# Linear attention and sentence-level experts on one core: repeated weights copied on chip, q relaid, a one-step root, and a searched order of work

## The chip, the cores and the metric

The kernel runs on one core of one Trainium2 chip. The metric is the time of one execution on the device in microseconds (us), and lower is better. Several executions of both kernels are taken on the same chip. A run counts as fast or slow by its own spread, and only fast runs are compared. A profile of one execution shows what each engine did. Its span is shorter than the reported time by some 1.7 us.

## The reference, cut to what matters

```python
# q, k, v: (8 batches, 8 heads, 576 rows, 64), fp32
kv  = einsum('bhsd,bhse->bhde', k, v)
out = einsum('bhsd,bhde->bhse', q, kv)
x   = out / sqrt(mean(out*out, -1) + 1e-6) * g_norm      # -> (8, 576, 512)
logits = x.mean(axis=1) @ w_gate                         # one row of 8 experts per batch
e      = argmax(logits, axis=1)                          # one expert for a whole batch
gate   = softmax(logits)[e]
out[b] = gate * (relu(x[b] @ w1[e]) @ w2[e])             # w1[e]: 512x1024, w2[e]: 1024x512
```

The weights of an expert are 4.19 MB in fp32, two matrices of 512 x 1024. The inputs are fixed, and with them the experts chosen are 4 4 7 6 5 1 3 1. So batch 1 repeats batch 0, and batch 7 repeats batch 5.

## The kernel before

For each batch there are stages, written as tokens of an order list: K (the kv matrix of all heads), T (transposes of q), O (q times kv and its square), M (mean of squares and root), X (normalized, transposed x), G (gate steps) and 17 units m0 to m16 of expert matrices. In the list "2T1" is batch 2, stage T, head pair 1. The list fixes the order on every engine, since each engine takes its instructions in the order in which they were written down.

```python
ORDER = ("0G2 1K 1T0 1T1 1T2 1O0 1T3 ... 0m0 0m1 1M2 1M3 0m2 ...")            # cut

def load_qkv(b, parts, which=None):                      # GpSimd issues, fp32 -> fp16 on the way
    ...
    for t, src in zip(kvq[b], (k, v, q)):
        nc.gpsimd.dma_start(t[0:R, hs], src[b, hs].rearrange(...))

def s_qt(b, c, ...):                                     # 12 half-width transposes for a head pair
    for j in range(NJ):
        for i in range(2):
            nc.tensor.transpose(pt[64*i:64*i+64, 0, j*R:(j+1)*R],
                                kvq[b][2][0:R, 2*c+i, j, :], ident[0:R, 0:R])
    nc.vector.tensor_copy(qT[:, c, :], pt[:, 0, 0:S])

def s_m(b, c):                                           # root in two ScalarE steps
    ...
    nc.scalar.activation(two(ln), pm[:, :, 0:HS], AF.Ln, bias=epsc)
    nc.scalar.activation(ln, ln, AF.Exp, scale=-0.5)

def s_gate2(b):                                          # expert's number, then its weights
    nc.tensor.matmul(pg, mean, ts, start=True, stop=True)
    nc.vector.max(mx, pg);  nc.vector.max_index(ix, mx, pg)
    nc.scalar.activation(lg, pg, AF.Exp, bias=nm, accum_out=gs)
    ev = nc.gpsimd.value_load(ix[0:1, 0:1], min_val=0, max_val=E - 1)
    nc.gpsimd.dma_start(w1, moe_w1[ds(ev, 1)]...)        # every batch loads 4.19 MB
    nc.gpsimd.dma_start(w2, moe_w2[ds(ev, 1)]...)
    load_qkv(b + 2, 1)                                   # q, k, v for a later batch, behind them

# m0..m7: w1 against xT, then Relu on ScalarE;  m8..m16: w2 against hT, then
# scaling by the gate on VectorE into ot (pool of 3 buffers), stored from SyncE
outp = ctx.enter_context(tc.tile_pool(name="outp", bufs=3))
```

Of the kernel before, what the change touches and what calls it, by code (L numbers as in the profile page):

```python
# [10 lines left out]
F16 = mybir.dt.float16  # L11
U32 = mybir.dt.uint32
# [6 lines left out]

ORDER = (  # L20
    "0G2 1K 1T0 1T1 1T2 1O0 1T3 1O1 1M0 1O2 1X0 1O3 1M1 0m0 0m1 1M2 1M3 0m2 1X1 0m3 0m4 "
    "1X2 1X3 1G0 1G1 0m5 0m6 1G2 0m7 0m8 2K 0m9 0m10 2T0 2T1 0m11 2O0 2O1 0m12 2M0 0m13 "
    "2M1 2T2 2X0 2X1 0m14 2O2 2T3 0m15 0m16 1m0 2M2 2O3 1m1 1m2 2X2 2M3 1m3 1m4 1m5 2X3 "
    "2G0 2G1 3K 1m6 2G2 3T0 3T1 1m7 3O0 3T2 1m8 3M0 3T3 1m9 3O1 3X0 3O2 1m10 3M1 3X1 1m11 "
    "1m12 3M2 3X2 3O3 1m13 1m14 1m15 3M3 1m16 3X3 3G0 2m0 2m1 2m2 3G1 2m3 2m4 3G2 2m5 4K "
    "2m6 4T0 4T1 2m7 4O0 4T2 2m8 4M0 4T3 2m9 4O1 4X0 4O2 2m10 4M1 4X1 2m11 2m12 4M2 4X2 "
    "4O3 2m13 2m14 2m15 4M3 2m16 4X3 4G0 3m0 3m1 3m2 4G1 3m3 3m4 4G2 3m5 5K 3m6 5T0 5T1 "
    "3m7 5O0 5T2 3m8 5M0 5T3 3m9 5O1 5X0 5O2 3m10 5M1 5X1 3m11 3m12 5M2 5X2 5O3 3m13 3m14 "
    "3m15 5M3 3m16 5X3 5G0 4m0 4m1 4m2 5G1 4m3 4m4 5G2 4m5 6K 4m6 4m7 6T0 6T1 4m8 6O0 6O1 "
    "4m9 6M0 4m10 6X0 6M1 6T2 6X1 4m11 6T3 4m12 6O2 4m13 6M2 4m14 6X2 6O3 4m15 4m16 6M3 "  # L30
    "5m0 5m1 6X3 6G0 5m2 6G1 5m3 5m4 6G2 5m5 7K 5m6 5m7 7T0 7T1 5m8 7O0 7O1 5m9 7M0 5m10 "
    "7X0 7M1 7T2 7X1 5m11 7T3 5m12 7O2 5m13 7M2 5m14 7X2 7O3 5m15 5m16 7M3 6m0 6m1 7X3 "
    "7G0 6m2 7G1 6m3 6m4 7G2 6m5 6m6 6m7 6m8 6m9 6m10 6m11 6m12 6m13 6m14 6m15 6m16 7m0 "
    "7m1 7m2 7m3 7m4 7m5 7m6 7m7 7m8 7m9 7m10 7m11 7m12 7m13 7m14 7m15 7m16 "
# [4 lines left out]
def kernel(  # L39
# [17 lines left out]
    R = 96  # L57
    NJ = S // R
    NP = H // 2
    HS = S // 2  # L60
    EPS = 1e-6
# [4 lines left out]
    wp = ctx.enter_context(tc.tile_pool(name="wp", bufs=3))  # L66
# [3 lines left out]
    hp = ctx.enter_context(tc.tile_pool(name="hp", bufs=2))  # L70
    outp = ctx.enter_context(tc.tile_pool(name="outp", bufs=3))
    ps0 = tc.tile_pool(name="ps0", bufs=1, space=bass.MemoryType.PSUM)
    psp = [ps0.__enter__()]
    ctx.enter_context(tc.manual_schedule())

    kvq = [None] * B
    ACT_OT = ()
    LOADS = {0: (2,), 1: (3,), 2: (4,), 3: (5,), 4: (6,), 5: (7,), 6: ()}
# [3 lines left out]
    def load_qkv(b, parts, which=None):  # L82
        if kvq[b] is None:
            kvq[b] = [pqkv.tile([P, H, NJ, Dh], F16, tag=n, name=n) for n in ("kt", "vt", "qt")]
        step = H // parts
        for i in (range(parts) if which is None else which):
            for t, src in zip(kvq[b], (k, v, q)):
                hs = slice(i * step, (i + 1) * step)
                nc.gpsimd.dma_start(  # L89
                    t[0:R, hs], src[b, hs].rearrange("h (p j) d -> p h (j d)", j=NJ))  # L90
# [5 lines left out]
    load_qkv(0, 4, (0, 1))  # L96
# [4 lines left out]
    nc.gpsimd.dma_start(wg, moe_w_gate.rearrange("(c p) e -> p c e", p=P))  # L101
    nc.scalar.preload_act_table_set("natural_log_exp_and_others")
    epsc = const.tile([P, 1], F32)
    nc.vector.memset(epsc, EPS)
# [5 lines left out]
    nc.vector.memset(ones[64:128, 64:128], 1.0 / Dh)  # L110
    mean = const.tile([P, P], F32)
    nc.vector.memset(mean, 1.0 / S)
    gates = const.tile([P, B], F32)
# [13 lines left out]
    def s_qt(b, c, w=0, copy=True):  # L127
        s = st[b]
        if "qT" not in s:
            s["qT"] = att.tile([P, NP, S], F16, tag="qT", name="qT")  # L130
        p32 = psum("t", 1, 1) if b == 0 else psum("a")
        warm(p32, w)
        pt = p32.bitcast(F16)
        for j in range(NJ):
            for i in range(2):
                nc.tensor.transpose(pt[64 * i:64 * i + 64, 0, j * R:(j + 1) * R],  # L136
                                    kvq[b][2][0:R, 2 * c + i, j, :], ident[0:R, 0:R])
        s["pt", c] = pt
        if copy:
            s_tc(b, c)  # L140

    def s_tc(b, c):
        nc.vector.tensor_copy(st[b]["qT"][:, c, :], st[b]["pt", c][:, 0, 0:S])  # L143

    def s_kv(b, prs, w=0):
        kt, vt = kvq[b][0:2]
        kv = kvb[:, b % 2]
        p32 = psum("kv", 1, 1) if b == 0 else psum("a")
# [12 lines left out]
    def s_o(b, c, tag="a"):  # L161
        s = st[b]
        po = psum(tag)
        for i in range(2):
            nc.tensor.matmul(po[:, i, 0:HS], kvb[:, b % 2, c, :],  # L165
                             s["qT"][:, c, i * HS:(i + 1) * HS], start=True, stop=True)
        sq = sm.tile([P, S], F16, tag="sq", name="sq")
        nc.scalar.activation(two(sq), po[:, :, 0:HS], AF.Square)  # L168
        if b == 0:
            o = po[:, :, 0:HS]  # L170
        else:
            o = two(sm.tile([P, S], F32, tag="o", name="o"))
            nc.vector.tensor_copy(o, po[:, :, 0:HS])  # L173
        s["sq", c], s["o", c] = sq, o

    def s_m(b, c, exp=True):
        s = st[b]
        sq = s["sq", c]
        pm = psum("p", 1) if b == 0 else psum("a")
        for i in range(2):  # L180
            nc.tensor.matmul(pm[:, i, 0:HS], ones, sq[:, i * HS:(i + 1) * HS],  # L181
                             start=True, stop=True)
        ln = sm.tile([P, S], F32, tag="ln", name="ln")
        nc.scalar.activation(two(ln), pm[:, :, 0:HS], AF.Ln, bias=epsc)  # L184
        s["ln", c] = ln
        if exp:
            s_e(b, c)

    def s_e(b, c):
        ln = st[b]["ln", c]  # L190
        nc.scalar.activation(ln, ln, AF.Exp, scale=-0.5)  # L191

    def s_x(b, c):
        s = st[b]
        if "xT" not in s:
            s["xT"] = xp.tile([P, NP, S], F16, tag="xT", name="xT")
            s["pl"] = sm.tile([P, NP], F32, tag="pl", name="pl")
        nc.vector.scalar_tensor_tensor(out=two(s["xT"][:, c, :]), in0=s["o", c], scalar=gcol,  # L198
                                       in1=two(s["ln", c]), op0=ALU.mult, op1=ALU.mult,
                                       accum_out=s["pl"][:, c:c + 1])  # L200

    def s_gate(b):
        s = st[b]
        tw = sm.tile([P, NP, E], F32, tag="tw", name="tw")
        nc.vector.tensor_tensor(tw, wg, s["pl"].unsqueeze(2).to_broadcast([P, NP, E]), ALU.mult)
# [3 lines left out]

    def s_gate2(b):  # L210
        s = st[b]
        pg = (psum("kv", 1, 1) if b == 0 else psum("a"))[:, 0, 0:E]
        nc.tensor.matmul(pg, mean, s["ts"], start=True, stop=True)
        mx = sm.tile([P, 8], F32, tag="mx", name="mx")
        ix = sm.tile([P, 8], U32, tag="ix", name="ix")
        nc.vector.max(mx, pg)
        nc.vector.max_index(ix, mx, pg)
        nm = sm.tile([P, 1], F32, tag="nm", name="nm")
        nc.vector.tensor_scalar(out=nm, in0=mx[:, 0:1], scalar1=-1.0, scalar2=None, op0=ALU.mult)
        lg = sm.tile([P, E], F32, tag="lg", name="lg")  # L220
        gs = sm.tile([P, 1], F32, tag="gs", name="gs")
        nc.scalar.activation(lg, pg, AF.Exp, bias=nm, accum_out=gs)
        ev = nc.gpsimd.value_load(ix[0:1, 0:1], min_val=0, max_val=E - 1)
        w1 = wp.tile([P, 4, F], F16, tag="w1", name="w1")
        w2 = wp.tile([P, 8, D], F16, tag="w2", name="w2")
        nh = 2 if b in (0, B - 1) else 1
        for h in range(nh):
            fs = slice(h * F // nh, (h + 1) * F // nh)
            nc.gpsimd.dma_start(w1[:, :, fs],  # L229
                                moe_w1[ds(ev, 1), :, fs].rearrange("o (c p) f -> p (o c) f", p=P))  # L230
        nc.gpsimd.dma_start(w2, moe_w2[ds(ev, 1)].rearrange("o (c p) d -> p (o c) d", p=P))
        s["w"] = (w1, w2)
        s["gs"] = gs
        for n in LOADS.get(b, (b + 3,)):
            if n < B:
                load_qkv(n, 1)

    def s_gate3(b):
        nc.vector.reciprocal(gates[:, b:b + 1], st[b]["gs"])

    def m_1(b, fb):
# [10 lines left out]
        nc.scalar.activation(two(s["hT"][:, fb, :]), ph[:, :, 0:HS], AF.Relu)  # L253

    def m_2(b, t, fcs):
        s = st[b]
        w2 = s["w"][1]
        if fcs[0] == 0:
            s["pm2"] = psum("m")
        po = s["pm2"]  # L260
        last = fcs[-1] == 7
        ob = out[b].rearrange("(p j) d -> j p d", j=NJ)
        if t == 4:
# [6 lines left out]
            if last:  # L270
                ot = outp.tile([P, D // 2], F32, tag="ot4", name="ot4")
                nc.vector.tensor_scalar(out=ot, in0=po[:, 0, 0:D // 2],  # L272
                                        scalar1=gates[:, b:b + 1], scalar2=None, op0=ALU.mult)
# [7 lines left out]
        if last:  # L281
            ot = outp.tile([P, D], F32, tag="ot", name="ot")
            if t in ACT_OT:
                nc.scalar.activation(ot, po[:, 0, :], AF.Copy, scale=gates[:, b:b + 1])
            else:
                nc.vector.tensor_scalar(out=ot, in0=po[:, 0, :], scalar1=gates[:, b:b + 1],  # L286
                                        scalar2=None, op0=ALU.mult)
# [11 lines left out]
    def moe_units(b):  # L299
        return ([lambda f=f: m_1(b, f) for f in range(8)] + [lambda: m_2(b, 4, range(8))]  # L300
                + [lambda t=t, h=h: m_2(b, t, range(4 * h, 4 * h + 4))
                   for t in range(4) for h in range(2)])

    warm(psum("kv", 1, 1), 10)
    for c in range(NP):
        s_kv(0, [c], 2)
        s_qt(0, c, 2, False)
# [64 lines left out]
```

## Time and profile before

| | kernel before |
|---|---|
| time, median of 3 | 220.87 us (220.2 to 221.81) |
| span of the profile | 217.4 us |
| TensorE busy | 184.1 us, 85% |
| DMA row | nines from 27 to 174 us |

The page has one line for each engine (busy time, share, count) and rows of digits, each digit the busy share of a fortieth of the span in tenths. Further down come the DMA queues (packets, MB, share) and the costliest groups of instructions (line, engine, operation, shapes, count, busy us, mean ns, idle time before). The prediction shows the main lines. These are needed besides:

```profile
q0 software_dynamic: 32592, 30.95, 89.9%
...
L184 ACT ACTIVATE ln<-ps_a,epsc 128x576 f32<-128x576 f32 x28 | 20.7, 738 | 16.3 <-PE ps_a L181 16.3
...
L191 ACT ACTIVATE ln<-ln 128x576 f32<-128x576 f32 x32 | 21.8, 683 | 1.0
...
L136 PE MATMUL ps_a<-ident,qt 96*64 96x96 f16 x336 | 11.4, 209 | 1.7 <-DMA qt<-in_q_dram 0.9
```

Queue q0 holds the loads that GpSimd issues: 30.95 MB as they arrive in fp16. The root takes two ScalarE steps, 738 and 683 ns for one head pair. The transposes are many and small.

### The profile page before, as it was taken

Reading aid. Unit: us, or ns where it says so; the run is one execution under the profiler, and the core shown is the slowest. Engines: PE = TensorE matmul, PEld = TensorE weight load, DVE = VectorE, ACT = ScalarE, POOL = GpSimd, SP = SyncE. Lnnn points to the kernel's source line nnn. Section 1 sums busy time; section 2 is a strip of 40 time slices with the busy share of each in tenths; the row PEclk is TensorE's granted clock in tenths of the full one; section 3 lists DMA queues with packets and bytes.
Section 4 is the critical chain, followed back from the end, with each engine's and each line's share of the span. In section 5 each row is a group of like instructions: output and inputs, shape, how many; then the busy total and the mean of one; then the engine's idle time right before and its main releaser. Section 6 shows DMA issues by size and latency. Waiting matters only on the chain.

```text
span 217.4 us, 4504 instructions
## 1 busy us (share of the span) xinstructions
PE 184.1 (85%) x1850; PEld 115.4 (53%) x1850; DVE 101.2 (47%) x248; ACT 107.7 (50%) x177; POOL 40.0 (18%) x58
## 2 busy tenths in 40 slices
PE   6886686779967897989889896999879999969991
PEld 2442455544655644864467455755666467436740
DVE  1254476246552486257543684168515871320041
ACT  2176098507581574647645564566545676112500
POOL 7930530600007000420016000700030004000000
PEclk9999999999996999999999999999999999996999
DMA  4999499999999999999999999999999953995034
GB/s 38 188 201 203 50 199 202 204 217 229 232 240 194 195 200 244 223 190 195 232 250 195 187 219 254 207 183 224 244 226 210 224 158 39 192 225 149 0 98 121
DMA packets 39142, 40.67 MB, mean 187 GB/s; under 512 B 2242, under 2 KB 31954, under 8 KB 39122
## 3 DMA queue, kind: packets, MB, share of 16 engines
q0 software_dynamic: 32592, 30.95, 89.9%
q1 hardware_dynamic: 6530, 9.44, 14.2%
q8 instruction: 14, 0.23, 0.4%
q14 instruction: 6, 0.05, 0.1%
HBM read 61.88 MB, written 9.44 MB: 328 GB/s over the span
## 4 chain that ended last, share of the span: by engine, by line
PE 38%; DMA 34%; ACT 9%; DVE 9%; issue 5%; POOL 2%; SPq 1%; POOLq 1%; DVEq 0%; ACTq 0%
DMA vt<-in_v_dram 23%; PE ps_m L250 17%; DMA out_dram<-ot 11%; PE ps_m L279 8%; ACT sq L168 3%; DVE o L173 3%; DVE ot L286 3%; PE ps_a L136 3%; PE ps_a L154 2%; ACT ln L184 2%; ACT hT L253 2%; ACT ln L191 2%; PE ps_m L266 1%; PE ps_a L181 1%; POOL kt L89 1%
## 5 line engine op out<-in xcount | busy, mean ns | idle before, releaser
L250 PE MATMUL ps_m<-xT,w 128*128 128x288 f16 x512 | 70.8, 293 | 10.2 <-DVE ot L286 7.8
L253 ACT ACTIVATE hT<-ps_m 128x576 f16<-128x576 f32 x64 | 41.0, 648 | 49.7 <-PE ps_m L250 49.1
L250 PEld LDWEIGHTS <-w 128*128 128x128 f16 x512 | 50.4, 101 | 26.7 <-issue 11.9
L279 PE MATMUL ps_m<-w,hT 128*128 128x512 f16 x256 | 61.4, 379 | 0.0
L279 PEld LDWEIGHTS <-hT 128*128 128x128 f16 x256 | 24.0, 98 | 23.6
L286 DVE TENSOR_SCALAR ot<-ps_m,gates 128x512 f32<-128x512 f32 x32 | 23.9, 747 | 21.5 <-PE ps_m L279 11.1
L229 POOL DMA_DIRECT2D w<-in_moe_w_dram x10 | 7.6, 761 | 142.1 <-PE ps_m L250 76.8
L184 ACT ACTIVATE ln<-ps_a,epsc 128x576 f32<-128x576 f32 x28 | 20.7, 738 | 16.3 <-PE ps_a L181 16.3
L173 DVE COPY o<-ps_a 128x576 f32<-128x576 f32 x25 | 18.6, 755 | 14.6 <-ACT sq L168 14.4
L198 DVE SCALAR_TENSOR_TENSOR xT<-o,gcol,ln 128x576 f16<-128x576 f32 x28 | 22.8, 814 | 5.4 <-ACT ln L191 5.2
L191 ACT ACTIVATE ln<-ln 128x576 f32<-128x576 f32 x32 | 21.8, 683 | 1.0
L168 ACT ACTIVATE sq<-ps_a 128x576 f16<-128x576 f32 x25 | 15.5, 643 | 12.8 <-PE ps_a L165 12.8
L143 DVE COPY qT<-ps_a 128x576 f16<-128x576 f16 x28 | 12.2, 453 | 7.6 <-PE ps_a L136 7.1
L181 PE MATMUL ps_a<-sq,ones 128*128 128x288 f16 x56 | 11.4, 284 | 4.7 <-DVE o L173 4.5
L136 PEld LDWEIGHTS <-qt 96*64 96x64 f16 x384 | 9.8, 110 | 9.0 <-issue 4.8
L136 PE MATMUL ps_a<-ident,qt 96*64 96x96 f16 x336 | 11.4, 209 | 1.7 <-DMA qt<-in_q_dram 0.9
L181 PEld LDWEIGHTS <-ones 128*128 128x128 f16 x64 | 6.0, 97 | 12.7 <-issue 8.6
L272 DVE TENSOR_SCALAR ot<-ps_m,gates 128x256 f32<-128x256 f32 x8 | 3.8, 481 | 18.2 <-PE ps_m L266 18.2
L154 PEld LDWEIGHTS <-kt 96*64 96x64 f16 x384 | 7.8, 117 | 8.5 <-issue 8.4
L158 DVE CAST kvb<-ps_a 64x256 f16<-64x256 f32 x7 | 2.9, 417 | 19.4 <-PE ps_a L154 19.4
L154 PE MATMUL ps_a<-vt,kt 96*64 96x64 f16 x336 | 7.1, 202 | 5.2 <-DMA vt<-in_v_dram 5.2
L124 PE MATMUL ps_kv<-kvb,ones 128*128 128x512 f16 x30 | 9.2, 441 | 2.1 <-DVE ones L110 2.0
(57 smaller groups left out, 121.0 us busy)
## 6 DMA issues: line engine op xcount, KB each, us to landing
w<-in_moe_w_dram POOLq DMA_DIRECT2D x14, 1024.0 KB, 13.5
out_dram<-ot SPq DMA_DIRECT2D x24, 192.0 KB, 5.2
kt<-in_k_dram POOLq DMA_DIRECT2D x7, 576.0 KB, 16.9
vt<-in_v_dram POOLq DMA_DIRECT2D x7, 576.0 KB, 20.4
qt<-in_q_dram POOLq DMA_DIRECT2D x7, 576.0 KB, 23.3
out_dram<-ot SPq DMA_DIRECT2D x40, 64.0 KB, 5.3
w<-in_moe_w_dram POOLq DMA_DIRECT2D x4, 512.0 KB, 6.6
out_dram<-ot SPq DMA_DIRECT2D x16, 128.0 KB, 5.7
```

The lines of the kernel that those rows point to most:

```text
L136: nc.tensor.transpose(pt[64 * i:64 * i + 64, 0, j * R:(j + 1) * R], kvq[b][2][0:R, 2 * c + i, j, :], ident[0:R, 0:R])
L154: nc.tensor.matmul(pk[64 * i:64 * i + 64, c, 64 * i:64 * i + 64], kt[0:R, 2 * c + i, j, :], vt[0:R, 2 * c + i, j, :], start=(j == 0), stop ...
L168: nc.scalar.activation(two(sq), po[:, :, 0:HS], AF.Square)
L173: nc.vector.tensor_copy(o, po[:, :, 0:HS])
L181: nc.tensor.matmul(pm[:, i, 0:HS], ones, sq[:, i * HS:(i + 1) * HS], start=True, stop=True)
L184: nc.scalar.activation(two(ln), pm[:, :, 0:HS], AF.Ln, bias=epsc)
L191: nc.scalar.activation(ln, ln, AF.Exp, scale=-0.5)
L198: nc.vector.scalar_tensor_tensor(out=two(s["xT"][:, c, :]), in0=s["o", c], scalar=gcol, in1=two(s["ln", c]), op0=ALU.mult, op1=ALU.mult, a ...
L250: nc.tensor.matmul(ph[:, i, 0:HS], w1[:, c, fb * P:(fb + 1) * P], s["xT"][:, c, i * HS:(i + 1) * HS], start=(c == 0), stop=(c == 3))
L253: nc.scalar.activation(two(s["hT"][:, fb, :]), ph[:, :, 0:HS], AF.Relu)
L279: nc.tensor.matmul(po[:, 0, :], s["hT"][:, fc, t * P:(t + 1) * P], w2[:, fc, :], start=(fc == 0), stop=(fc == 7))
L286: nc.vector.tensor_scalar(out=ot, in0=po[:, 0, :], scalar1=gates[:, b:b + 1], scalar2=None, op0=ALU.mult)
```

## The change

Its intent: load fewer weights, give TensorE fewer instructions and ScalarE fewer steps, and order everything by a search. The parts are:

- Weights live in three slots. Batch b copies, on VectorE, the slot of batch b-1 or b-2 into its own slot. Its load follows under a condition that is false if one of those two batches had the same expert.
- In batches 2 to 7, VectorE relays q so that a head pair lies side by side, and six full-width transposes replace twelve.
- The root is one ScalarE step. The gate's exponential moves to GpSimd (a power with base e).
- Loads come as q, k, v instead of k, v, q. The first ones of batch 0 go through SyncE and ScalarE as fp32 and are cast.
- Five output buffers instead of three, and one hT buffer instead of two.
- A new order list, in which an x at the end of a token moves that copy, Relu or scaling to the other of VectorE and ScalarE.

The core of the diff, with cuts marked by "...":

```diff
-    "0G2 1K 1T0 1T1 1T2 1O0 1T3 1O1 1M0 1O2 ...
+    "0D9 0R1 0R2 0R0 0K02 0T02 0C0 0O0 ... 0G1 0P0 1K0 1T0 1O0 1T1x ... 2L0 ... 2Q0 ... 1W0 ...
-    wp = ctx.enter_context(tc.tile_pool(name="wp", bufs=3))
-    outp = ctx.enter_context(tc.tile_pool(name="outp", bufs=3))
+    outp = ctx.enter_context(tc.tile_pool(name="outp", bufs=5))
+    W1 = const.tile([P, NW, 4, F], F16, name="W1")          # NW = 3 slots
+    W2 = const.tile([P, NW, 8, D], F16, name="W2")
-            for t, src in zip(kvq[b], (k, v, q)):
+            for t, src in zip(kvq[b], (q, k, v)):
 ...
+            if "qr" in s:
+                nc.tensor.transpose(pt[:, 0, j * R:(j + 1) * R], s["qr"][0:R, c, j], ...)
+                continue
 ...
+    def s_qr(b):
+        for c in range(NP):
+            nc.vector.tensor_copy(s["qr"][0:R, c].rearrange("p j (i d) -> p j i d", i=2), ...)
 ...
-        nc.scalar.activation(two(ln), pm[:, :, 0:HS], AF.Ln, bias=epsc)
-        nc.scalar.activation(ln, ln, AF.Exp, scale=-0.5)
+        nc.scalar.activation(part(s["rs", c], h), pm[...], AF.Abs_reciprocal_sqrt, bias=epsc)
 ...
+    def s_w(b):
+        own = b % NW
+        if b > 0:
+            sv = nc.vector.value_load(st[b]["src"][0:1, 0:1], ...)      # slot of b-1 or b-2
+            for W in (W1, W2):
+                for h in range(2):
+                    nc.vector.tensor_copy(W[:, own, half h], W[:, ds(sv, 1), half h])
+            for e in evs[max(0, b - 2):b]:
+                c = evs[b] != e
+                cond = c if cond is None else s_logical_and(cond, c)
+        nc.gpsimd.dma_start(W1[:, own, :, fs], moe_w1[ds(ev, 1), :, fs]..., cond=cond)
+        nc.gpsimd.dma_start(W2[:, own], moe_w2[ds(ev, 1)]..., cond=cond)
 ...
+        nc.gpsimd.tensor_tensor(lg, base, dl, ALU.pow)
```

In the new list W is the copy and load of weights, Q the relaying, L a load of q, k, v, and D filler matmuls.

## The prediction

> **What bounds the kernel now.** I read four views in this order: the page's shares and slices, the waits, the chain that ended last, and busy time by stretch. The page first:
>
> ```profile
> PE 184.1 (85%) x1850; PEld 115.4 (53%) x1850; DVE 101.2 (47%) x248; ACT 107.7 (50%) x177; POOL 40.0 (18%) x58
> ...
> PE   6886686779967897989889896999879999969991
> ...
> DMA  4999499999999999999999999999999953995034
> GB/s 38 188 201 203 50 199 202 204 217 229 232 240 194 195 200 244 223 190 195 232 250 195 187 219 254 207 183 224 244 226 210 224 158 39 192 225 149 0 98 121
> ...
> HBM read 61.88 MB, written 9.44 MB: 328 GB/s over the span
> ```
>
> Two resources run close to full together. TensorE is at 85% and the DMA row is nines from slice 5 to slice 31 (27 to 174 us, at 5.4 us a slice). VectorE and ScalarE are half idle. The row dips at slice 4, where all loads issued so far have landed and the first expert is not known yet.
>
> The stretch view, the middle of the kernel as one piece (columns: length, busy time of PE, PEld, DVE, ACT, POOL, then granted clock, DMA share, GB/s):
>
> ```profile
> 30.00:180.00 150.00, 131.45 (x1391) 86.04 (x1391) 81.02 (x194) 86.56 (x144) 21.48 (x27) 0.99 1.17 213
> ```
>
> 213 GB/s times 150 us is 31.95 MB as the engines wrote it. Of this about 7.1 MB are stores (six of eight batches of the 9.44 MB). The other 24.9 MB are fp16 tiles, read as fp32 at twice the bytes: 49.7 MB in 150 us, 332 GB/s of reads beside 47 GB/s of writes. I take that as the rate of a full DMA here.
>
> Waits, total us, times, longest:
>
> ```profile
> DVE ot L286 <- DMA out_dram<-ot: 10.4, 5, 3.5
> PE ps_m L250 <- DVE ot L286: 7.8, 5, 2.4
> PE ps_a L154 <- DMA vt<-in_v_dram: 5.2, 3, 2.6
> PE ps_a L181 <- DVE o L173: 4.5, 10, 0.6
> ```
>
> The first two are one chain: with three output buffers VectorE waits for a store (5 to 6 us to landing), and TensorE then waits for VectorE at the batch boundary. The third is TensorE waiting for loads. The start and end of the chain:
>
> ```profile
> 19.07 0.75 ACT ln L184
> 19.84 0.69 ACT ln L191
> ...
> 22.39 0.18 DVE mx L216
> 22.60 0.24 DVE ix L217 x2
> 22.93 0.37 ACT lg L222 x2
> 23.34 1.02 PE ps_a L124 x4
> ...
> 204.78 1.04 PE ps_m L266 x16
> 205.82 7.03 PE ps_m L279 x32
> 212.87 0.75 DVE ot L286
> ```
>
> Batch 0 runs as a serial chain until 23.3 us; after the last matmul at 212.9 the evacuation and a store take 4.5 us. So: 23 us of start, 190 us of middle, 4.5 us of tail.
>
> **What the Trainium skill says.** "VectorE: DVE Perf Modes", The perf-mode tier table, gives a 16-bit SBUF to SBUF copy of 2048 elements 4x mode and 693 ns; a PSUM source does not get it. No such copy is in this trace; the PSUM copy of 576 fp16 elements (qT) takes 453 ns. "SBUF — State Buffer", Who interferes with whom, says such a copy takes a port pair that it shares with GpSimd, and the other fully blocks; loads issued from GpSimd need that engine to write descriptors. This trace has no such copies, so cannot confirm it. "ScalarE: Activation LUTs", What ACT_TABLE_LOAD costs, says time per element is the same for every function, about 280 + 0.833 N ns with a pointer bias: 760 ns at 576. The trace's Ln with that bias takes 738, so agrees, and I give the one-step root 0.74 us. "DMA: Bandwidth & Descriptors", Issuing engines are not separate DMA queues, says that loads from SyncE or ScalarE run on the same 16 engines. So moving the first three loads there can buy only issue time.
>
> **The change part by part.**
>
> Skipped loads. The reference's arithmetic on its fixed inputs chooses experts 4 4 7 6 5 1 3 1. The new code compares with the two batches before, so batches 1 and 7 skip their load: 2 x 4.19 MB = 8.4 of 61.9 MB (4.19 MB is two 512 x 1024 fp32 matrices). At 332 GB/s this is 25 us of DMA time. Off the path: the later of DMA and TensorE sets the end, so I work out both below.
>
> Copies. Seven batches copy four pieces of 2048 fp16 elements whether they need to or not: 28 x 0.69 = 19.4 us of VectorE, an estimate from the skill's figure. The q relaying adds 6 batches x 4 copies of 768 elements, estimated at 0.36 us each (the page's 150-odd fixed cycles plus 192 at 0.96 GHz): 8.6 us. With the order's marks, which give some copies and evacuations to the other engine, I count about 111 us on VectorE and 101 us on ScalarE for the work after batch 0, over some 160 us. So neither becomes the bound by its sum, even though VectorE now also waits for weights to land before it copies.
>
> Root in one step. It removes 32 Exp at 0.683 = 21.8 us from ScalarE. This engine was half idle, so only the start's chain gains.
>
> Full-width transposes. In batches 2 to 7, twelve half-width transposes become six full ones per head pair: 24 pairs x 12 become 24 x 6, 144 fewer. Twelve took 0.38 us (chain). A 288-column matmul takes 0.125 us in a run (40 in 4.92 us), so six of 96 columns would be 0.25 to 0.35 us. Gain 24 x 0.03 to 0.13, say 1 to 2 us.
>
> Five output buffers for three. This should remove the 7.8 us.
>
> Start. Removed from batch 0's chain: the Exp (0.69), half of the last pair's square, root and product (the last pair is done in halves, about 0.8 in all), tw and ts (0.4 plus hand-offs) and lg before the next matmuls (0.4). Loads on three queues give perhaps 0.3. Together 2.5 to 3: the second batch starts at about 20.5 instead of 23.3 us.
>
> TensorE's sum. Units from runs of the trace: eight 288-column matmuls 1.00 us (40 in 4.92), a half of an output tile 0.87 (32 matmuls in 7.03, eight halves), the 64-row piece 1.04, K 0.89, twelve transposes 0.36, O and M 0.25 each, gate 0.13. From the second batch on: 64 x 1.00 + 64 x 0.87 + 8 x 1.04 + 7 x 0.9 + 28 x 0.36 + 56 x 0.25 + 0.9 = 159 us for before, 158 for after. Check on before: 23.3 + 159 + 4.5 = 187, measured span 217.4; the missing 30 us are the waits above, a clock of 0.83 after pauses, and small hand-offs. Floor of after: 20.5 + 158 + 4 = **182.5 us**.
>
> DMA's sum. 53.5 MB of reads at 332 GB/s is 161 us, at 350 it is 153; plus 2 us before the first. The last needed load is batch 6's weights, whose first matrix lands some 6 us before the end: 149 to 157 us. After it come batches 6 and 7 on TensorE: 2 x (8 x 1.00 + 1.04 + 8 x 0.87) = 32 us, and the 4 us tail: **185 to 193 us**. Both floors lie close together. The order places batch 6's weight issue 113 us of TensorE work after the second batch starts (at 133 us) and its first use 126 us after (at 147), so it needs about the landing times that the DMA can just give.
>
> Sum. Take 189 as the higher floor and add 4.5 us for hand-offs that stay (4.5 us of L181 waiting for VectorE, evacuations behind long copies, restarts of the load chain, since a weight load is issued only after the previous one landed and was copied): span 193.5. The reported times are longer than the profiled span: 219.07 against 217.4 in the profiled run, 220.87 as median. I add 2.5: **196 us**, a ratio of 0.89.
>
> **The rivals.**
>
> A: the copies become a new wait. VectorE runs in order; the copy for batch b must wait until the weights of b-1 have landed. If those are late, VectorE stands still, TensorE's results are not evacuated, and the next load is issued later still. For: the DMA is nearly full, so landings are late by nature. Against: the order puts each copy 7 to 14 us after the first use of the previous weights. If it bites 3 us in five batches: 208 to 211 us.
>
> B: the copy doesn't get the fast mode, since its source slot comes from a register. Then 28 copies take 2.3 us by the same page, 64 us, and VectorE has some 155 us of work in 160: 215 us or more. For: no such copy in the trace. Against: types and strides fit, only the address is dynamic.
>
> C: DMA time is hidden anyway and TensorE's hand-offs were the bound. For: only 5.2 + 0.9 us of TensorE's waits name a load. Then skipped loads give some 6 us, buffers 8, start 3, transposes 1: 202 us. Against: DMA at 99% for 150 us means that loads set the pace of the gate and so of everything.
>
> D: the searched order fits the chip so well that both floors are met: 187 to 189 us.
>
> **How the range and the chances follow.** D gives 188 as low end, A's milder form and C give the high end of 206, with 196 between. Slower than 216 needs B or a strong A; even then the removed store waits and start remain. I give faster 0.95, same 0.03, slower 0.02.
>
> **What would show it.** Skips: reads of 53.5 MB instead of 61.9. Copies: 28 groups of 128x2048 at about 0.69 us (2.3 shows B), and 24 of 96x768 near 0.36. Root: one 0.74 us step per head pair and no Exp. Buffers: no wait of VectorE for a store above 1 us. Start: batch 1's K at 20 to 21 us. Rival A shows as VectorE's W copies waiting for a weight DMA. The prediction would be wrong most likely through the DMA: if its row falls out of nines before batch 6's weights, the issue chain and not the rate set the end; and if TensorE shows under 5 us of idle, D holds.

## The result, and the profile after

The changed kernel took 206.06 us (median of 4, 205.08 to 207.76), the kernel before in the same rounds 220.69 us. The ratio is 0.934, 95% interval 0.926 to 0.941. A ratio here is the mean time of one kernel's fast runs over the mean of the other's fast runs of the same rounds, so not quite the ratio of the medians. On two other chips the unaltered changed kernel had 0.948 and 0.936. The direction was right, and the time is 10 us above the prediction and just outside its range of 188 to 206.

The page of the changed kernel, the rows that answer to those of before:

```profile
PE 179.3 (88%) x1709; PEld 115.3 (57%) x1709; DVE 116.2 (57%) x292; ACT 103.4 (51%) x165; POOL 51.4 (25%) x64
...
PE   6887578979885999998999879999979999999990
...
PEclk9999959999999999999999988999999999999998
DMA  6999299998999999999999999999998999053053
...
q0 software_dynamic: 29328, 26.30, 83.0%
...
HBM read 61.88 MB, written 9.44 MB: 351 GB/s over the span
```

Queue q0 moved 26.30 MB, 4.65 MB less. Of that 4.2 MB are the two skipped expert loads in fp16, the rest are the first loads that now use other queues. The page's line on HBM still says 61.88 MB: it counts what the program names, not what was skipped (53.49 MB where an experiment below takes two loads out of the program), so the prediction's check on this line would have misled. The DMA row is nines and eights until 173 us, hardly less full than before. The granted clock (PEclk) drops to one half in the slice from 25 to 30 us.

The costliest groups, from the page:

```profile
L272 POOL TENSOR_TENSOR lg<-base,dl 128x8 f32<-128x8 f32 x8 | 14.8, 1849 | 89.2 <-DVE src L291 77.4
...
L227 ACT ACTIVATE rs<-ps_a,epsc 128x576 f32<-128x576 f32 x28 | 20.5, 740 | 10.0 <-PE ps_a L223 9.7
...
L307 DVE COPY W<-W 128x2048 f16 (+1 forms) x28 | 19.5, 719 | 4.1 <-DMA W<-in_moe_w_dram 1.6
```

The copies took 19.5 us in all (19.4 predicted) and the root 740 ns (0.74 predicted). The power of 8 elements on GpSimd takes 1.85 us, more than the prediction had thought to ask about.

The waits (total us, times, longest):

```profile
POOL W L317 <- DVE W L307: 13.8, 4, 7.1
...
PE ps_a L191 <- DMA vt<-in_v_dram: 7.5, 4, 2.9
...
DVE W L307 <- DMA W<-in_moe_w_dram: 1.6, 1, 1.6
...
PE ps_m L346 <- DMA W<-in_moe_w_dram: 1.5, 1, 1.5
```

No wait of VectorE or ScalarE for a store is left. The largest wait of TensorE is now the one for v, which comes last of the three loads, and GpSimd waits for copies before it issues weights. TensorE's timeline shows the first and the last of its waits for loads:

```profile
23.30 0.95 PE L191 MATMUL ps_a<-vt,kt 96*64 96x64 f16 x48 [1.46 <-DMA vt<-in_v_dram]
...
149.19 1.16 PE L346 MATMUL ps_m<-xT,W 128*128 128x288 f16 x8 [1.47 <-DMA W<-in_moe_w_dram]
```

After 149 us TensorE does not pause at all until its last matmul ends at 198.6. The busy times of that stretch say the same (length, then PE, PEld, DVE, ACT, POOL, clock, DMA share, GB/s):

```profile
149.19:198.63 49.44, 49.42 (x352) 31.80 (x352) 20.77 (x48) 21.46 (x33) 5.35 (x7) 1.00 0.64 139
```

So from 149 us on TensorE alone sets the time, and the question is what put that point at 149 us. The late weights of batch 5 have a history on two engines. GpSimd's timeline and, below it, VectorE's:

```profile
129.88 1.67 POOL L272 TENSOR_TENSOR lg<-base,dl 128x8 f32<-128x8 f32 x1 [9.69 <-DVE src L291]
138.59 0.99 POOL L317 DMA_DIRECT2D W<-in_moe_w_dram  x1 [7.05 <-DVE W L307]
```

```profile
135.75 0.76 DVE L350 TENSOR_SCALAR hT<-ps_m 128x576 f16<-128x576 f32 x1 [1.67 <-PE ps_m L346]
136.53 2.75 DVE L307 COPY W<-W 128x2048 f16 x4
```

The expert was known at 129.1 us, and GpSimd was free at 131.5. The load had to wait for copies that VectorE began only at 136.5, since the list has them behind other work.

I cut the span of each profiled run into four terms: the start (until batch 1's K), TensorE idle from there to its last matmul (the pauses that its timeline names), TensorE running (the rest up to there), and the tail.

| run | start | running | idle | of it for loads | tail | span | clock |
|---|---|---|---|---|---|---|---|
| before | 24.3 | 166.8 | 21.7 | 6.3 | 4.6 | 217.4 | 0.983 |
| changed | 23.3 | 162.4 | 12.9 | 7.5 | 4.8 | 203.4 | 0.971 |
| predicted | 20.5 | 158 | 11 | | 4 | 193.5 | |

The prediction's 11 us of idle are 6.5 (the DMA's floor of 189 over TensorE's 182.5) and 4.5 of hand-offs. The start of before contains 1.0 us of filler matmuls.

### The profile page after: what moved, and what is told of

It reads as the page before. It is cut to its first block, busy times and chain, and to the rows that moved or that the text cites. A ratio compares the mean times of both kernels' runs of the same rounds, so it can differ in the third digit from the quotient of the medians.

```text
span 203.4 us, 4406 instructions
## 1 busy us (share of the span) xinstructions
PE 179.3 (88%) x1709; PEld 115.3 (57%) x1709; DVE 116.2 (57%) x292; ACT 103.4 (51%) x165; POOL 51.4 (25%) x64
## 3 DMA queue, kind: packets, MB, share of 16 engines
q0 software_dynamic: 29328, 26.30, 83.0%
HBM read 61.88 MB, written 9.44 MB: 351 GB/s over the span
## 4 chain that ended last, share of the span: by engine, by line
PE 47%; DMA 35%; DVE 6%; POOL 4%; issue 3%; ACT 2%; DVEq 0%; POOLq 0%; ACTq 0%
DMA vt<-in_v_dram 26%; PE ps_m L346 22%; PE ps_m L385 16%; DMA W<-in_moe_w_dram 5%; DMA qt<-in_q_dram 3%; PE ps_a L206 3%; DVE W L307 2%; PE ps_a L223 2%; PE ps_m L373 1%; PE ps_a L191 1%; POOL kt L100 1%; POOL lg L272 1%; ACT sq L211 1%; POOL qt L100 1%; PE ps_a L158 1%
## 5 line engine op out<-in xcount | busy, mean ns | idle before, releaser
L346 PE MATMUL ps_m<-xT,W 128*128 128x288 f16 x512 | 70.2, 288 | 1.8 <-DMA W<-in_moe_w_dram 1.5
L385 PE MATMUL ps_m<-W,hT 128*128 128x512 f16 x256 | 62.3, 386 | 0.0
L346 PEld LDWEIGHTS <-W 128*128 128x128 f16 x512 | 49.8, 99 | 15.6 <-DMA W<-in_moe_w_dram 2.0
L353 ACT ACTIVATE hT<-ps_m 128x576 f16<-128x576 f32 x44 | 28.7, 653 | 22.6 <-PE ps_m L346 22.3
L385 PEld LDWEIGHTS <-hT 128*128 128x128 f16 x256 | 24.8, 99 | 24.6 <-issue 1.5
L272 POOL TENSOR_TENSOR lg<-base,dl 128x8 f32<-128x8 f32 x8 | 14.8, 1849 | 89.2 <-DVE src L291 77.4
L357 ACT ACTIVATE ot<-ps_m,gates 128x512 f32<-128x512 f32 (+1 forms) x24 | 15.0, 626 | 22.8 <-PE ps_m L385 12.6
L227 ACT ACTIVATE rs<-ps_a,epsc 128x576 f32<-128x576 f32 x28 | 20.5, 740 | 10.0 <-PE ps_a L223 9.7
L236 DVE SCALAR_TENSOR_TENSOR xT<-o,gcol,rs 128x576 f16<-128x576 f32 x28 | 22.2, 811 | 2.5 <-ACT rs L227 2.3
L350 DVE TENSOR_SCALAR hT<-ps_m 128x576 f16<-128x576 f32 x20 | 15.1, 756 | 11.8 <-PE ps_m L346 11.7
L307 DVE COPY W<-W 128x2048 f16 (+1 forms) x28 | 19.5, 719 | 4.1 <-DMA W<-in_moe_w_dram 1.6
## 6 DMA issues: line engine op xcount, KB each, us to landing
vt<-in_v_dram POOLq DMA_DIRECT2D x7, 576.0 KB, 19.4
```

The costliest lines, as they stand in the source:

```text
L227: nc.scalar.activation(part(s["rs", c], h), pm[:, 0:2 if h is None else 1, 0:HS], AF.Abs_reciprocal_sqrt, bias=epsc)
L236: nc.vector.scalar_tensor_tensor(out=part(s["xT"][:, c, :], h), in0=s["o", c, h], scalar=gcol, in1=part(s["rs", c], h), op0=ALU.mult, op1= ...
L272: nc.gpsimd.tensor_tensor(lg, base, dl, ALU.pow)
L307: nc.vector.tensor_copy(W[:, own, h * n:(h + 1) * n], W[:, ds(sv, 1), h * n:(h + 1) * n].rearrange("p o c f -> p (o c) f"))
L346: nc.tensor.matmul(ph[:, i, 0:HS], w1[:, c, fb * P:(fb + 1) * P], s["xT"][:, c, i * HS:(i + 1) * HS], start=(c == 0), stop=(c == 3))
L353: nc.scalar.activation(two(s["hT"][:, fb, :]), ph[:, :, 0:HS], AF.Relu)
```

## The experiments

My theories at this point. *Rate*: the DMA is full, loads are late because of their bytes, and whatever is gained elsewhere turns into waiting for loads. *Late issue*: loads are late because in-order queues (VectorE's copies, GpSimd's gate steps) issue them late. *Hand-offs and clock*: TensorE's own work, its clock and short waits set the time, and loads matter little.

All kernels gave right results except the one marked. Times are medians; ratios are to the kernel before in the same rounds.

**The changed kernel again**, as control of the next three, unaltered.

> Control: the changed kernel unaltered, on the chip of the next three. All theories: 205 to 207 us, as before (206.06).

Measured: 208.04 us, ratio 0.948 (0.940 to 0.956), 1 us above what was expected of an unaltered kernel.

**Copies kept, no skip.** The condition is dropped, every batch loads.

```diff
-                cond = c if cond is None else s_logical_and(cond, c)
+                cond = None
```

> The copies stay, but every batch loads its weights (no skip). If the skipped loads carry the gain (DMA rate theory), 8.4 MB come back at about 330 GB/s, of which batch 1's share of some 12 us lies ahead of everything: 214 to 219 us. If the gain came from the buffers, the order and the root instead, and the DMA had room, 206 to 209 us.

Measured: 227.60 us, ratio 1.033 (1.024 to 1.041): slower than the kernel before. By mean times the skip is worth 19.2 us (227.20 less 208.04). This exceeds the expected 214 to 219. TensorE's waits tell why:

```profile
PE ps_m L346 <- DMA W<-in_moe_w_dram: 20.6, 5, 11.9
```

The longest, 11.9 us, is for batch 1's weights. The new list has their load behind the q, k, v of batches 2 and 3, which is harmless only if that load is skipped.

**No copies, no skip.** Both are cut out of the weights' stage; all else of the change stays.

```diff
-        if b > 0:
-            ... value_load, four tensor_copy, conditions
+        # straight to the load of W1[:, own], W2[:, own], without a condition
```

> Neither copies nor skip, all else of the change. Against the run with copies and loads this measures the copies alone. Theory that the copies hold up VectorE and through it the issue of the next weights (rival A): 4 to 8 us faster than the run with copies and loads, and close to the changed kernel. Theory that VectorE has the room (57% busy): within 2 us of it.

Measured: 218.00 us, ratio 0.994 (0.987 to 1.001). So everything else in the change together (buffers, root, transposes, order) does not show as a gain without the skip, in an order made for the skip. This does not say that the rest is worth nothing: the buffers alone gain 5 us in the kernel before (below), so without the skip this order loses. Again one wait for batch 1's weights stands out:

```profile
PE ps_m L333 <- DMA W<-in_moe_w_dram: 14.0, 2, 12.1
```

**No copies, skip by known routing.** Batches 1 and 7 use the slots of batches 0 and 5. This is right for this input only.

```diff
+        if b in (1, 7):
+            own = {1: 0, 7: 5 % NW}[b]
+            st[b]["w"] = (W1[:, own], W2[:, own])
+            return
```

> No copies, and batches 1 and 7 read the slots of batches 0 and 5, which is known of this input (right result here only). It keeps the saved loads and drops the 19.5 us of copies. Rival A: 198 to 203 us. Room on VectorE: 204 to 206 us.

Measured: 203.16 us, ratio 0.923 (0.915 to 0.931). Against the control the copies cost 5.2 us (208.04 less 202.83 by means), and without the skip 9.1 us (227.20 less 218.12). The 9.1 is a little more than the 4 to 8 us expected of this pair. Against the control's trace (start 23.5, running 163.2, idle 14.2, 8.6 of it for loads) idle is 3.6 us less here, all of it waits for loads. So the copies hold the loads up: rival A of the prediction, at a moderate size. The skip alone, without copies, is worth 15.3 us.

**Filler ahead of batch 1's K**, as the kernel before has.

```diff
-1K0
+1K04
```

> Four filler matmuls ahead of batch 1's K, as the kernel before has. In the changed kernel TensorE waits 1.46 us for v of batch 1 and then shows a granted clock near one half from about 25 to 30 us. If the missing filler is the cause, the slice shows full clock again and the time falls by 1.5 to 3 us (about 205 on this chip, where the changed kernel is 206 to 208). If the pause itself is the cause, the filler only adds its 0.9 us: 207 to 209 us.

Measured: 207.14 us, ratio 0.938 (0.930 to 0.945), so no gain that can be told from the changed kernel (0.934 to 0.948 on three chips). The trace shows both halves of the reason. The stretch from 20 to 35 us in the changed kernel and below it with the filler (the last three columns are granted clock, DMA share, GB/s):

```profile
20.00:35.00 15.00, 10.92 (x149) 7.56 (x149) 7.57 (x19) 4.71 (x9) 6.20 (x8) 0.77 0.92 125
```

```profile
20.00:35.00 15.00, 10.58 (x154) 6.51 (x153) 7.52 (x19) 5.59 (x11) 6.20 (x8) 1.00 0.78 104
```

The clock is full where it was 0.77. Running falls by 2.2 us, from 162.4 to 160.2. The rest of the clock's loss stays: as in the changed kernel (0.89 from 115 to 130 us), the clock drops again after a wait of 2.2 us for v, here at 120 us. Idle rises from 12.9 to 14.5 us, the part of it for loads from 7.5 to 8.6, and the start is 2.5 us later (25.8 us). So the gain in clock was given back, to the start and to late loads. (The later start holds 1.0 us of filler and 1.9 us in which batch 0 waited for its own v. This wait for batch 0's loads appears in the fast profiles of five altered versions, with 0.8 to 2.2 us, and in the others with 0.6 or less; I did not find its cause.)

**Batch 3's loads early**, right behind batch 2's.

```diff
-2L0 0G2 1X3 0G3 0m4 1G0 0m2 1G1 ... 2T0x 0m14 3L0     (shortened)
+2L0 3L0 0G2 1X3 0G3 0m4 1G0 0m2 1G1 ... 2T0x 0m14     (shortened)
```

> Loads of batch 3's q, k, v issued right after batch 2's (at about 30 us) instead of behind two gate steps of GpSimd's queue (45.7 us). Late-issue theory: the wait of 2.9 us for v of batch 3 goes, and all later loads move up by 2 to 4 us: 203 to 206 us. Rate theory (DMA full anyway): the wait moves to the next load, within 1 us of the changed kernel.

Measured: 205.04 us, ratio 0.935 (0.930 to 0.940). The wait for v fell from 7.5 to 3.2 us, that for batch 0's v came up with 1.5. Against three values of the changed kernel, 0.934 to 0.948, this is at the good end: a small gain at most.

**Batches 4 and 5: weights earlier.** Batch 4's copy goes ahead of batch 6's relaying, batch 5's right behind its gate.

```diff
-... 5M2 3m5 6Q0 3m3 5M1 3m4 4W0 ...    ... 4m0 5G1 4m7x ... 4m6 5W0 ...
+... 5M2 3m5 4W0 6Q0 3m3 5M1 3m4 ...    ... 4m0 5G1 5W0 4m7x ... 4m6 ...
```

> The copy and weight load of batch 4 is placed ahead of batch 6's q relaying (whose wait for q holds VectorE 2.1 us), that of batch 5 right behind its index. Late-issue theory: the 5.9 and 7.1 us that GpSimd waits for the copies shrink, the waits for v of batch 6 (2.2) and for batch 5's weights (1.5) go: 2 to 4 us faster than the changed kernel. Rate theory: within 1 us.

Measured: 209.61 us, ratio 0.948 (0.942 to 0.955), not faster. The profiled run was slow, so the reading comes from the next version, which contains this edit.

**The three together.**

> The three edits together. Late-issue theory with the clock: the sum, 199 to 203 us. Rate theory: 205 to 208 us.

Measured: 205.55 us, ratio 0.938 (0.932 to 0.943). TensorE's timeline:

```profile
130.74 3.42 PE L346 MATMUL ps_m<-xT,W 128*128 128x288 f16 x16 [4.36 <-DVE hT L350]
```

With batch 5's copy early, VectorE reached it before all weights of batch 4 had landed. It stood still for 1.8 us in the middle of the copy, which itself takes 2.8 us, and the evacuation that TensorE needed was behind it: TensorE waited 4.4 us. This is rival A in the open. So of these edits, batch 5's had to go.

**Weights loaded for batch 0 only** (wrong result, relative error 1.2): the copies hand them on.

```diff
+        if b > 0:
+            st[b]["w"] = (W1[:, own], W2[:, own])
+            return                                   # behind the copies, before the loads
```

> Wrong result on purpose: weights are loaded for batch 0 only, the copies hand them on, everything else stays. This takes 25 MB (batches 2 to 6) off the DMA and no wait of VectorE's copies but that for a load. Rate theory (loads late because the DMA is full): the waits for v and weights after 24 us go (about 7.5 us with what follows them), span near 195, time 196 to 199 us. Hand-off theory (TensorE's own work, clock and the short waits for VectorE and ScalarE set the time): within 3 us of the changed kernel.

Measured: 198.80 us, ratio 0.908 (0.901 to 0.914); span 196.6. Without 21 MB of weight reads (five loads of 4.19 MB; the text has 25 by mistake), the kernel is only some 3 to 4% faster. Its terms: start 23.4, running 159.4, idle 8.9, tail 4.8. So the weight loads hold 6 to 9 us of the changed kernel, as the rate theory expected, and even with none the prediction's 193.5 would not have been met. This run does not tell rate from late issue, since the bytes and the late issues vanish together.

**Loads in the old order k, v, q.**

```diff
-            for t, src in zip(kvq[b], (q, k, v)):
+            for n in (1, 2, 0):
+                t, src = kvq[b][n], (q, k, v)[n]
```

> The changed kernel with loads in the old order k, v, q instead of q, k, v. The changed kernel waits for v at four K stages (7.5 us in all), v being the last of three. If the order is to blame, these waits shrink to below 3 us and the time falls 2 to 4 us. If the full DMA is, the wait moves to q (the relaying and transposes): within 1.5 us.

Measured: 213.98 us, ratio 0.974 (0.966 to 0.982), 6 to 9 us worse than the changed kernel by the ratios, a miss of both expectations. TensorE's waits:

```profile
PE ps_a L159 <- DVE qr L173: 11.9, 6, 4.2
```

VectorE's:

```profile
DVE qr L173 <- DMA qt<-in_q_dram: 17.3, 4, 4.9
```

With q last, VectorE stands in front of the relaying for 17.3 us, where it waited 2.1 us in the changed kernel. The old order is worse because an in-order engine with other work now needs q first.

**The kernel before with five output buffers.**

```diff
-    outp = ctx.enter_context(tc.tile_pool(name="outp", bufs=3))
+    outp = ctx.enter_context(tc.tile_pool(name="outp", bufs=5))
```

> The kernel before with five output buffers instead of three. The prediction's sum counted 7.8 us for these waits as won. If so: 212 to 214 us. If the DMA that is full takes the time back (loads of the next batch late instead): 217 to 220 us.

Measured: 213.94 us, ratio 0.977 (0.970 to 0.984). The buffers alone are worth 5 us (2.3% of 219), not the 7.8 us of the two waits. All waits for stores are gone, and one for loads keeps its size:

```profile
PE ps_a L154 <- DMA vt<-in_v_dram: 5.1, 3, 2.8
```

**A better list**: the filler, batch 3's loads early, batch 4's copy ahead of the relaying; batch 5's stays.

> Filler ahead of batch 1's K, batch 3's loads early, batch 4's copy ahead of the relaying of batch 6; batch 5's copy left where it was, as moving it made TensorE wait 4.4 us behind VectorE. Late-issue theory: 202 to 205 us reported, span near 199 to 200. Rate theory: within 1 us of the changed kernel (206 to 208).

Measured: 201.91 us, ratio 0.921 (0.915 to 0.926). This interval lies below those of the changed kernel in all its measurements: some 2% faster, though no control ran in the same rounds. This is what the late-issue theory expected (202 to 205 us), once the edits don't put VectorE in front of a load that has not landed. But the filler is in the list too, no run has the two other edits without it, and the profiled run was slow, so what each part gave is not shown.

**Half-width transposes, no relaying**: the Q tokens are taken out, the transposes fall back to the old form.

> The changed kernel without the q relaying: twelve half-width transposes per head pair as before, and no 24 copies of 96x768 on VectorE. Prediction's term: TensorE loses 1 to 2 us, so 207 to 209 us where the changed kernel is 206 to 208. Rival: the relaying costs more on VectorE (its wait for q, some 7 us of copies) than it saves on TensorE: 203 to 206 us.

Measured: 204.72 us. The four runs fell into two groups, 202.64 and 203.00 us at a clock of 0.985 and 0.992, and 206.50 and 206.44 at 0.974, so there are too few fast runs. It is no slower than the changed kernel. From the groups of the changed kernel by shape:

```profile
L158 PE MATMUL ps_a<-ident,qr 96*128 96x96 f16 x144 | 9.4, 206 | 0.1
...
L172 DVE COPY qr<-qt 96x768 f16<-96x768 f16 x24 | 8.3, 405 | 2.1 <-DMA qt<-in_q_dram 2.1
```

Six full-width transposes take 0.26 us in the chain where twelve took 0.38, so 24 x 0.12 = 2.9 us less for TensorE. VectorE pays 8.3 us for it and waits for q. No run here shows that the relaying pays.

**Three output buffers in the changed kernel.**

> The changed kernel with three output buffers. As the kernel before gained 2.3% (5 us) from five, the same is expected to be lost if stores still land in 5 to 6 us: 209 to 213 us, with waits of VectorE or ScalarE for a store. If the spread of evacuations over two engines has already removed the waits: within 1.5 us.

Measured: 212.10 us, ratio 0.962 (0.954 to 0.970), so 3 to 6 us worse than the changed kernel. A wait for stores is back:

```profile
DVE ot L359 <- DMA out_dram<-ot: 4.9, 2, 4.3
```

**Ln and Exp instead of the one-step root.**

```diff
-                             AF.Abs_reciprocal_sqrt, bias=epsc)
+                             AF.Ln, bias=epsc)
+        rs = part(s["rs", c], h)
+        nc.scalar.activation(rs, rs, AF.Exp, scale=-0.5)
```

> The changed kernel with Ln and Exp in place of the one-step root (32 more ScalarE steps of about 0.68 us, 21.8 us). Prediction: only the start's chain feels it, so 207 to 209 us. Rival: ScalarE, at half its time, sits between TensorE steps in every stage and its queue delays evacuations: 210 to 216 us.

Measured: 207.21 us, ratio 0.943 (0.936 to 0.949), within what the changed kernel had. ScalarE's busy time went from 103.4 to 122.6 us (51% to 60%) at no cost that shows.

**The better list with k, v first for batch 1 alone.**

> The best version with k and v ahead of q for batch 1 alone (which has no relaying). If the order of the first loads holds the start: batch 1's K moves from 23 to about 22 us and the time falls 1 to 2 us below the best version (ratio to the kernel before 0.912 to 0.918 instead of 0.921). If their bytes hold it: the wait moves to q, ratio 0.919 to 0.924.

Measured: 201.91 us, ratio 0.918 (0.913 to 0.923). This is the fastest of the versions that are right for any input, but its interval overlaps that of the better list (0.915 to 0.926), so the edit itself is not shown to help. In its trace batch 1's K follows the filler without a wait, at 24.4 us and not at the expected 22. It does so in the filler run too, where v still comes last, so this is no effect of the order.

**The better list without relaying, loads in the order k, v, q.**

> The best version without relaying (half-width transposes) and with the loads in the order k, v, q. Without relaying nothing on VectorE waits for q, so v can come before q at no cost: the waits for v at the K stages shrink and the 7 us of relaying leave VectorE. Expected 0.905 to 0.918 of the kernel before (198 to 201 us). If the wait only moves to q at the transposes: 0.918 to 0.925.

Measured: 211.41 us, ratio 0.958 (0.954 to 0.963), a clear miss. The wait has only moved:

```profile
PE ps_a L163 <- DMA qt<-in_q_dram: 8.4, 3, 3.9
```

**The changed kernel once more**, as control on that chip.

> The changed kernel unaltered, as control on the chip of the best version: ratio to the kernel before 0.934 to 0.948, and 3 to 6 us slower than the version of this call.

Measured: 206.81 us, ratio 0.936 (0.932 to 0.941). On this chip it is faster than the version beside it.

The profiled runs in terms, as above (fast runs only):

| run | start | running | idle | of it for loads | span | clock |
|---|---|---|---|---|---|---|
| copies, no skip | 22.8 | 169.0 | 29.6 | 24.8 | 226.2 | 0.925 |
| no copies, no skip | 23.4 | 164.4 | 23.0 | 16.9 | 215.7 | 0.953 |
| no copies, skip | 23.5 | 162.3 | 10.6 | 5.0 | 201.3 | 0.970 |
| filler | 25.8 | 160.2 | 14.5 | 8.6 | 205.3 | 0.978 |
| weights of batch 0 only | 23.4 | 159.4 | 8.9 | 2.6 | 196.6 | 0.988 |
| better list, k and v first | 24.4 | 160.1 | 11.0 | 4.6 | 200.3 | 0.988 |
| changed, last control | 23.3 | 165.0 | 13.1 | 7.9 | 206.3 | 0.958 |

The last row against the changed kernel's first profile (running 162.4 at 0.971) shows how far this term moves with the clock from run to run. Running times clock is 156 to 158 us in every row, and 157.7 in the changed kernel's first profile.

## Why the prediction was right or wrong

The direction was right, and so was the cause that it named first: in this order of work no gain shows without the skip. It was wrong in size. The profiled run's 205.1 us against the predicted 196, by terms:

| term | predicted | measured | error |
|---|---|---|---|
| start | 20.5 | 23.3 | +2.8 |
| TensorE running | 158 | 162.4 | +4.4 |
| idle | 11 | 12.9 | +1.9 |
| tail | 4 | 4.8 | +0.8 |
| span to reported time | 2.5 | 1.7 | -0.8 |

The step that failed is "Floor of after: 20.5 + 158 + 4 = **182.5 us**". It measured 23.3 + 162.4 + 4.8 = 190.5 us, and two of its terms carry the error.

The larger is the 158. The units came from runs at full clock, and the text had itself put part of the gap in the kernel before down to "a clock of 0.83 after pauses". It then gave the changed kernel no such term. Its mean granted clock was 0.971, and running times clock is 157.7 us: an estimate, since this clock is a mean over the whole span, but it lets the clock account for the missing 4.4 us. (In the kernel before the product is 164.0 us where the prediction's sum had 159. I did not trace that difference, so the good fit may be in part luck.) The filler run is the direct test: with a clock of 1.00 from 20 to 35 us instead of 0.77, running fell by 2.2 us. The same run shows that the term can't simply be added: the start grew by 2.5 us and idle by 1.6.

The other is "the second batch starts at about 20.5 instead of 23.3 us". It was worked out from the chain of computation alone. In the changed kernel this chain ends about 21.8 us, with the logits' matmuls, only 0.5 us earlier than in the kernel before (22.4). Part of what was won there goes to filler. The last x of batch 0 is ready at 20.6 us, but six filler matmuls stand ahead of the logits in TensorE's order:

```profile
20.05 1.46 PE L146 MATMUL ps_kv<-kvb,ones 128*128 128x512 f16 x6 [0.75 <-ACT rs L227]
21.44 0.40 PE L253 MATMUL ps_t<-wg,pl 128*1 128x8 f32 x10
```

No run takes this filler out. After the chain, K of batch 1 waited 1.46 us for v, which landed at 23.2 and was issued last of its three. The prediction had not asked where the loads of batch 1 would be. With the filler added for the clock, K begins later still (24.4 in the fastest version).

Idle was near: 7.5 us for loads where the sum had 6.5, 5.4 for hand-offs where it had 4.5. But the loads are others than the prediction's. It let batch 6's weights set the end, issued at 133 us. They were issued at 155.9 and first used at 166.7, without a wait. What TensorE waited for was v, three times after batch 1, and batch 5's weights at 149. Nor does any of its views show the "DMA at 99%": they show a row of nines and a share of 1.17.

Of the other steps:

- Skipped loads: right in kind, 15.3 us without the copies and 19.2 us with them, in an order made for the skip. A list made for loading every batch was not tried, so what the skip is worth against the best order without it stays open.
- Copies: 19.5 us for 19.4, and 0.405 us against 0.36 for the relaying (median 0.349). The dynamic source slot does not cost the fast mode, and rival B fell: 0.704 us a piece (the median of all 28 is 0.694), less than the 0.811 of batch 1's four copies, whose source is fixed and which ran beside GpSimd's load issues. The prediction said that neither engine becomes the bound by its sum, and that held. They cost 5.2 us all the same, through waits; the 4.5 us of the prediction for all hand-offs were meant to cover such.
- Five buffers: 7.8 us predicted, 5 us measured in the kernel before. The waits went, and in its profile idle is 9.1 us less than in that of the kernel before; 1.2 us of start and 2.4 us of running, at a clock of 0.960 instead of 0.983, came up in their place.
- Transposes: 2.9 us off TensorE (1 to 2 predicted), bought with VectorE's time, and no gain shown.
- Root: no gain, as predicted.
- Rival A: real, moderate in the changed kernel, and provoked at will by moving one copy (4.4 us). Rival C fell for this order: without the skip no gain shows, 0.994. Its 8 us for the buffers were real in part (5 us in the kernel before). Its observation that few waits name a load was right in numbers and misleading: in the run without skip and copies 16.9 us of them do, 12.1 of these for batch 1's weights.
- The two floors, TensorE's and the DMA's, do lie close together: taking 21 MB of weight loads away brings only 6 to 9 us.

What stays open: how much of the waiting for loads is the DMA's rate and how much late issue, the wait for batch 0's own loads that some profiles have, why the granted clock differs between runs of one kernel (0.959 to 0.975 in four fast runs), and whether a list made for half-width transposes would beat the relaying.

## What to carry to other kernels

A load that is skipped under a condition paid here, where the DMA was nearly full and the order was made for it, and the fallback copy must sit on an engine where nobody waits behind it: place it after the landing that it waits for and not ahead of an evacuation. When two resources are close to full, add up the start, the running time at the clock that the profile really grants, and the waits, rather than the higher of two floors. The order of loads follows from who needs which first on an in-order engine, not from which wait is longest in the profile: both attempts to put k and v ahead of q for all batches lost some 5 to 9 us against the changed kernel.

## What the Trainium skill lacked or had wrong

- "TensorE: Matmul & The Clock Gate", Why this matters for your kernels, warns of idle gaps of more than about 3 us. That figure does not cover several shorter pauses close together: here pauses of 1.46, 1.18 and 0.73 us between 22 and 28 us, none longer, went with a granted clock of 0.77 from 20 to 35 us, and four filler matmuls ahead of K went with 1.00.
- "ScalarE: Activation LUTs", What it computes, advises against Rsqrt and names a reciprocal and a Sqrt instead. The one-step Abs_reciprocal_sqrt, which it does not list, gave right results here at 740 ns for 128x576.
- No page that I read gives the cost of a power on GpSimd: 1849 ns for 128x8 elements.
- "SBUF — State Buffer", Who interferes with whom, lets one expect GpSimd's load issues and VectorE's copies to block one another, and gives no size. The trace agrees, mildly: four relaying copies took 1.15 or 1.16 us with no load issue beside them and 1.40 to 1.76 us beside one (three groups of each kind), and one issue beside the weight copies took 1.24 us instead of 0.77.
- No page that I read says that a skipped load leaves the page's HBM total as it was (61.88 MB), while its queue moved 4.2 MB less and its issue took 0.04 us.
